# VectorE transposes in place of DRAM bounces, inverses by pairs of blocks, 768-wide weight conversion, and blocks 0 and 1 through the FFN together

## The chip, the cores and the metric

The kernel runs on one core of a Trainium2 chip. The metric is the device time of one execution in microseconds (us); lower is better. TensorE appears in the profile as PE (matmuls) and PEld (loads of the stationary operand), VectorE as DVE, ScalarE as ACT, GpSimd as POOL. SP issues most of the DMAs and ACT issues some; all of them go out through queues to the same 16 DMA engines.

## The reference

Four sequences of 768 tokens with 8 heads of dimension 48 go through a delta rule. For each head, from state 0 (48 x 48) and token by token:

```python
k_n = k / (np.linalg.norm(k, axis=-1, keepdims=True) + 1e-06)
for t in range(S):
    y[:, :, t] = np.einsum('bhd,bhde->bhe', q[:, :, t], state)
    v_old = np.einsum('bhde,bhd->bhe', state, kt)
    state = state + bt[:, :, :, None] * np.einsum('bhd,bhe->bhde', kt, vt - v_old)
```

Then the 3072 outputs of width 384 go through an FFN: `h = x @ w_in` (384 x 2048), a leaky ReLU with slope 0.01, and `@ w_out` (2048 x 384). The weights come as float64, all else as float32.

## The kernel before

**Blocks.** Time is cut into 12 blocks of 64 tokens; a block holds all 32 (sequence, head) pairs, in two groups g of 16. Within a block the recurrence is solved in closed form. `gram(n)` multiplies keys by keys and by queries (tile pg). The key products make, for each of the 32 heads and each half of 32 tokens, a triangular 32 x 32 system L. `norms` and `inv` scale and invert it: `eliminate` takes one of 31 columns per step, with a product into tmp (L263) and a subtraction from T (L268) on VectorE, all 128 partitions at once. `merge` puts the inverses T into the tile rt and builds the coupling of the two halves (matmuls pz and pu). `solve(n)` then runs pk, pw, py (the block's outputs) and pc (the new state). `columns(n)` transposes the outputs into xh and xl, a high and a low part.

**The bounces.** The Gram matrix lies with tokens on partitions, and the inverse needs heads on partitions. So `gram` writes 32 x 32 pieces to DRAM (gd, L209) and reads them back (L, L224). The inverse goes back the same way: td and tt are written (L307, L308) after an ACT copy Tt (L299), and rt and gm are read (L318, L320). For blocks 0 and 1 these DMAs go out on ACT's queue, later on SP's.

**Inverses.** Blocks 0 and 1 are inverted together: two halves times 32 heads times two blocks fill the 128 partitions. Every later block is inverted alone, with the columns of T split over the two halves of the partitions (16 instead of 32 columns, 31 steps).

**FFN.** `ffn(n)` takes the 256 tokens of a block in 16 units f. A unit is nine matmuls ph (w_in chunk f, three splits times three column chunks), an activation gh and ph on ACT (L472, L473), the low part gl on DVE (L475), and six matmuls po with the w_out chunk, two units later.

**Weights.** Each of the 32 half chunks of 384 columns arrives as raw 64-bit words (wr) and is taken apart into a high and a low float by seven DVE operations (L148 to L161) and two ACT ones. Six half chunks are converted ahead of everything else, the other 26 within the FFN of block 0.

**Order.** All of this is Python generators; `weave` says how many steps of solve, inverse, Gram and weights belong to each unit of the FFN, and a scheduler then fixes one order of instructions per engine. Every engine works in that order. Ahead of block n's FFN, its solve must be done; within it run solve(n+1), the inverse of n+2 and the Gram matrix of n+3.

Of the kernel before, what the change touches and what calls it, by code (L numbers as in the profile page):

```python
# [19 lines left out]
D = 48  # L20
C = 64
# [26 lines left out]
def delta_moe_kernel(ctx: ExitStack, tc, kqT, kv, qT, beta, cst, w_all, out, nblk):  # L48
# [33 lines left out]
    NR = dict(k=KT_BUFS, q=Q_BUFS, t=KT_BUFS, v=2 * NGR)  # L82
    ring = {x: [st.tile([P, 2, GU, C if x in "qt" else D], F32, name=f"r{x}{i}") for i in range(NR[x])] for x in NR}
    UP, DN = slice(0, D), slice(R0, P)

    NB = [[0, 1]] + [[n] for n in range(2, nblk)]
    where = {n: (b, i) for b, ns in enumerate(NB) for i, n in enumerate(ns)}

    def of(x, n, g):
        return ring[x][(n * NGR + g) % NR[x]]  # L90

    def statics():
        nc.scalar.dma_start(csb, cst)
        for t in ring["t"]:
            nc.vector.memset(t, 0.0)
        for x in "vq":
            for t in ring[x]:
                nc.gpsimd.memset(t[0:R0], 0.0)
# [27 lines left out]

    def weights():
# [3 lines left out]
        for k in range(2 * NFC):  # L131
            f, x = k // 2, k % 2
            words = raws.pop(k).bitcast(F32).rearrange("p (n two) -> p two n", two=2)
            lo, hi = words[:, 0], words[:, 1]
            loi, hii = lo.bitcast(U32), hi.bitcast(U32)
            g = sb.tile([P, DO], F32, tag="cg", name=f"cg{k}", bufs=CB)
            r = sb.tile([P, DO], F32, tag="cr", name=f"cr{k}", bufs=1)
            gi, ri = g.bitcast(U32), r.bitcast(U32)

            def final():  # L140
                t = sb.tile([P, 2 * DO], F32R, tag=f"w{k}", name=f"w{k}", bufs=1)
                for e in range(2):
# [12 lines left out]
            nc.vector.scalar_tensor_tensor(gi, hii, 0xC0000000, gi, ALU.bitwise_and, ALU.bitwise_or)
            nc.vector.tensor_scalar(ri, hii, 0x1FF, 14, ALU.bitwise_and, ALU.logical_shift_left)
            nc.vector.scalar_tensor_tensor(ri, loi, 18, ri, ALU.logical_shift_right, ALU.bitwise_or)  # L157
            nc.vector.tensor_scalar(e.bitcast(U32), gi, 0xFF800000, None, ALU.bitwise_and)
            d0, d1 = final()
            nc.scalar.copy(d0, g)  # L160
            nc.vector.scalar_tensor_tensor(d1, ri, 2.0 ** -34, e, ALU.mult, ALU.mult)  # L161
# [8 lines left out]
    def dq(n):  # L170

        return nc.scalar if n < 2 else nc.sync


    def gram(n):
        if n * NGR >= Q_BUFS:
            need(sv, solve, n - Q_BUFS // NGR)
        kqs = []
        for g in range(NGR):
            t = sb.tile([P, GS, NPAIR, 2, C], F32, tag="kq", name=f"kq{n}_{g}", bufs=KQ_BUFS)  # L180
            kqs.append(t)
            with behind("L"):
                for b in range(2):
                    (nc.sync, nc.scalar)[b if n < 2 else 0].dma_start(
                        t[b * R0:b * R0 + D].rearrange("p s u x t -> p (s u x t)"), kqT[n, g, b])
        b0, i = where[n]
        if i == 0:
            Lh[b0] = sb.tile([P, HC, HC], F32, tag="L", name=f"L{b0}", bufs=2)
        gd = dr.tile([64, HC, HC], F32, tag="gd", name=f"gd{n}")
# [408 lines left out]
```

## Time and profile before

| quantity | value |
|---|---|
| median of three runs | 725.47 us (725.08 to 725.88) |
| profiled execution: its own span | 722.7 us |
| busy: PE / DVE / ACT / POOL | 625.2 / 499.3 / 323.5 / 7.3 us |
| start to end of the first inverse (blocks 0 and 1) | 43.4 to 64.6 us |
| first matmul ph of the FFN | 95.8 us |
| FFN of block 2 under way | from 230.5 us |
| blocks 3 to 8, one period | 51.3 us |

The profile gives the profiled execution's own time only as its span, from the first to the last instruction; the times of the three runs are measured from outside. The prediction quotes the rows. A row of the groups by line reads: line, engine, operation, out<-in and shape, count, then busy us and mean ns of one, then idle time of the engine just before them and what ended it. A row of the chain of waits reads: start, length, what. A row of the timeline adds engine and line, and in brackets the idle time before. A row of the table by stage reads: stretch, its length, and the busy us of PE, PEld, DVE, ACT, POOL with counts, the granted TensorE clock, the DMA share and GB/s.

### The profile page before, as it was taken

The page shows a single profiled execution, that of the slowest core. Times are in us where ns is not written, and L with a number is a line of the kernel's source. Part 1 is how long each engine was busy: PE and PEld are TensorE (multiplying, and loading weights), DVE is VectorE, ACT ScalarE, POOL GpSimd, SP SyncE. Part 2 cuts the span into 40 slices and gives each one's busy share as a digit, 9 for nine tenths or more (in the row PEclk, how much of TensorE's full clock was granted, in tenths as well). Part 3 has the DMA queues.
Part 4 walks back from the last instruction along what each step waited for, and adds up shares of the span by engine and source line. Part 5 has one row for each costly group of instructions (what it writes and reads, how often), then busy time and mean ns, then how long its engine had stood idle before and what let it go on. Part 6 is the DMA issues. An engine that isn't in the chain of part 4 may idle for free.

```text
span 722.7 us, 20972 instructions
## 1 busy us (share of the span) xinstructions
PE 625.2 (87%) x8296; PEld 580.9 (80%) x8296; DVE 499.3 (69%) x2222; ACT 323.5 (45%) x830; POOL 7.3 (1%) x12
## 2 busy tenths in 40 slices
PE   4200689978996999999999999999999999999996
PEld 4200569967995998988989999989989989999996
DVE  7988998999594856956955947847758559531211
ACT  3211554733453453554454544534634635544332
POOL 4000000000000000000000000000000000000000
PEclk9999978988997999999999999999999999999999
DMA  9594785250306437036055063072171260410000
GB/s 239 102 271 107 177 206 131 59 115 23 46 14 128 85 57 164 4 68 154 3 98 124 3 128 95 15 136 73 32 142 49 50 129 2 68 24 2 3 20 23
DMA packets 130786, 60.91 MB, mean 84 GB/s; under 512 B 115392, under 2 KB 118592, under 8 KB 130688
## 3 DMA queue, kind: packets, MB, share of 16 engines
q1 hardware_dynamic: 117376, 56.81, 35.4%
q10 hardware_dynamic: 13312, 2.76, 2.3%
q8 instruction: 65, 1.06, 0.6%
q14 instruction: 33, 0.27, 0.1%
HBM read 46.96 MB, written 12.58 MB: 82 GB/s over the span
## 4 chain that ended last, share of the span: by engine, by line
PE 65%; DVE 18%; DMA 7%; ACT 4%; SPq 3%; issue 3%; ACTq 0%; DVEq 0%
PE ph L468 26%; PE po L458 23%; PE pw L396 3%; PE pk L383 3%; DVE rq L216 3%; DMA tt<-T 3%; DVE rv L388 2%; DVE T L268 2%; PE pu L342 2%; DVE tmp L263 2%; DMA wr<-in_w_all 2%; PE py L414 2%; PE pz L334 2%; PE px L443 1%; SPq L307 1%
## 5 line engine op out<-in xcount | busy, mean ns | idle before, releaser
L468 PE MATMUL ph<-xh,w 128*128 128x256 f32 x1152 | 255.6, 295 | 11.4 <-DVE gl L475 8.2
L468 PEld LDWEIGHTS ph<-xh,w 128*128 128x128 f32 x1152 | 195.1, 192 | 22.5 <-DVE gl L475 11.4
L458 PE MATMUL po<-w,gh 128*128 128x384 f32 x768 | 188.0, 342 | 2.4 <-ACT gh L472 2.4
L475 DVE TENSOR_TENSOR gl<-ph,gh 128x256 fp32r<-128x256 f32 x192 | 80.4, 422 | 132.4 <-ACT ph L473 123.4
L468 PE MATMUL ph<-xl,w 128*128 128x256 f32 x576 | 165.9, 289 | 1.6 <-DVE xl L116 0.9
L472 ACT ACTIVATE gh<-ph 128x256 fp32r<-128x256 f32 x192 | 73.5, 383 | 171.2 <-PE ph L468 170.1
L458 PEld LDWEIGHTS po<-w,gh 128*128 128x128 f32 x768 | 132.3, 190 | 4.3 <-ACT gh L472 4.0
L458 PE MATMUL po<-w,gl 128*128 128x384 f32 x384 | 118.8, 343 | 1.5 <-DVE gl L475 1.4
L468 PEld LDWEIGHTS ph<-xl,w 128*128 128x128 f32 x576 | 110.7, 192 | 4.4 <-DVE xl L116 3.5
L268 DVE TENSOR_TENSOR T<-T,tmp 128x60 f32<-128x60 f32 (+35 forms) x661 | 112.0, 206 | 1.3
L263 DVE TENSOR_TENSOR tmp<-T,L 128x60 f32<-128x60 f32 (+35 forms) x661 | 111.9, 206 | 0.7
L473 ACT ACTIVATE ph<-ph 128x256 f32<-128x256 f32 x192 | 73.1, 380 | 0.0
L458 PEld LDWEIGHTS po<-w,gl 128*128 128x128 f32 x384 | 68.0, 191 | 2.4 <-DVE gl L475 1.9
L334 PE MATMUL pz<-rt,gm 32*32 32x32 f32 x768 | 19.7, 196 | 39.8 <-DMA rt<-td 39.7
L201 PE MATMUL pg<-kq 48*64 48x128 f32 x768 | 39.8, 313 | 13.2 <-DMA kq<-in_kqT 10.0
L334 PEld LDWEIGHTS pz<-rt,gm 32*32 32x32 f32 x768 | 15.9, 111 | 42.7 <-DMA rt<-td 39.9
L201 PEld LDWEIGHTS pg<-kq 48*64 48x64 f32 x768 | 32.0, 154 | 19.8 <-DMA kq<-in_kqT 10.8
L216 DVE TENSOR_TENSOR rq<-pg,csb 64x256 f32<-64x256 f32 x96 | 40.6, 423 | 2.2 <-ACT gs L205 0.5
L443 PE MATMUL px<-csb,ys 128*128 128x128 f32 x144 | 25.9, 299 | 8.1 <-DVE rq L216 5.1
L160 ACT CAST w<-cg 128x384 fp32r<-128x384 f32 x32 | 16.3, 511 | 36.8 <-DVE cr L157 26.5
L385 ACT ACTIVATE rt<-pk 48x512 f32<-48x512 f32 x44 | 26.1, 593 | 14.2 <-PE pk L383 13.4
L280 DVE MEMSET T<- 128x512 f32 (+1 forms) x11 | 5.8, 524 | 38.1 <-DMA tt<-T 37.9
(61 smaller groups left out, 650.3 us busy)
## 6 DMA issues: line engine op xcount, KB each, us to landing
wr<-in_w_all SPq DMA_DIRECT2D x32, 384.0 KB, 4.9
kq<-in_kqT SPq DMA_DIRECT2D x44, 192.0 KB, 3.6
L<-gd SPq DMA_DIRECT2D x22, 256.0 KB, 3.9
rk<-in_kv SPq DMA_DIRECT2D x24, 192.0 KB, 3.3
rv<-in_kv SPq DMA_DIRECT2D x24, 192.0 KB, 4.2
rq<-in_qT SPq DMA_DIRECT2D x24, 192.0 KB, 3.8
out<-ob SPq DMA_DIRECT2D x48, 96.0 KB, 2.6
gd<-gs SPq DMA_DIRECT2D x88, 32.0 KB, 2.7
```

The costliest lines, as they stand in the source:

```text
L201: nc.tensor.matmul(ps[b][c * 64:(c + 1) * 64, p * 128:(p + 1) * 128], kq[r, c ^ b, p, 0], kq[r, c ^ b, p].rearrange("p x t -> p (x t)"), s ...
L216: nc.vector.tensor_tensor(qa[DN, c, b * NPAIR:(b + 1) * NPAIR], pv[b][r, 1], tri[r].rearrange("p (o t) -> p o t", o=1).broadcast_to([C, NP ...
L263: nc.vector.tensor_tensor(tv, t[:, :, j:j + 1].broadcast_to([P, k, w]), L[:, j, j + 1:].rearrange("p (o w) -> p o w", o=1).broadcast_to([P ...
L268: i = nc.vector.tensor_tensor(t, t, tv, ALU.subtract)
L334: nc.tensor.matmul(zv[h * 64:h * 64 + HC, u], gt[lo, l], t[lo, h, u, HC:], start=True, stop=True)
L385: nc.scalar.mul(t[UP, c], pv[c * 64:c * 64 + D], -1.0)
L443: nc.tensor.matmul(x[:, g * P:(g + 1) * P], ys[n, g][:, cc * P:(cc + 1) * P], eye, start=True, stop=True)
L458: i = nc.tensor.matmul(po[t][:, :DO], a[:, ts_], w[f], start=(f == 0 and k == 0), stop=(f == NFC - 1 and k == 2))
L468: nc.tensor.matmul(ph, a[f][:, cc * P:(cc + 1) * P], x[cc][e], start=(k == 0), stop=(k == 3 * NCC - 1))
L472: nc.scalar.activation(gh, ph, AF.Prelu, alpha=0.01)
L473: i = nc.scalar.activation(ph, ph, AF.Prelu, alpha=0.01)
L475: i = nc.vector.tensor_tensor(gl, ph, gh.bitcast(F32), ALU.subtract)
```

## The change

**Transposes.** The DRAM tiles gd, td and tt and their DMAs are gone. `gram` copies the key products into one SBUF tile S, and `turn` transposes it by 32 x 32 blocks on VectorE into L (four instructions of 32 x 1024 for two blocks). `merge(n)` does the same with T: two such instructions into rt, one into gm. All heads of rt are one tile now. `merge` is one step ahead of the two `join`s, which hold what was left of the old merge.

**Pairs.** Grams and inverses go by pairs of blocks (0,1), (2,3) and so on, six inverses in all, each as wide as the first one was before. The inverse of a pair is laid into the FFN of the even block before it (31 of 33 steps at units 5 to 17), its Gram matrix into units 0 to 4. For the first two pairs the key products come first and the query products (pq) in a second pass, with tiles that lie in weight slots not yet filled.

**Weights.** A chunk f is one load of 768 KB and one conversion 768 wide: seven DVE operations instead of fourteen, two of which work on 16-bit parts of the words. The gates say which conversions may go ahead: behind the first merge for f up to 2, behind block 0's columns for the others. No weight is converted before the first inverse.

**FFN.** Blocks 0 and 1 run together, unit by unit, block 1 four units behind block 0, so that a chunk serves both; the FFN therefore begins with both solves due first, in the order that `weave` gives. Set-up fills and the identity copies move from VectorE to GpSimd.

```diff
-    NR = dict(k=KT_BUFS, q=Q_BUFS, t=KT_BUFS, v=2 * NGR)
+    NR = dict(k=K_BUFS, q=Q_BUFS, v=2 * NGR)
+    rt = st.tile([P, HS, C], F32, name="rt")
...
     def weights():
-        for k in range(2 * NFC):
+        for f in range(NFC):
+            with behind("S0"):
+                nc.scalar.activation(g, hi.bitcast(F32), AF.Abs)
+            with behind(gate):
+                if f >= WU:
+                    nc.vector.tensor_copy(r16[:, 0], part[:, 1])
+                nc.vector.tensor_scalar(r16[:, 1], part[:, 2], 0x1FF, None, ALU.bitwise_and)
+                nc.vector.tensor_scalar(g, g, HI_MIN, HI_MAX, ALU.max, ALU.min)
             nc.vector.tensor_scalar(gi, gi, 3, 0x3FFFF000, ALU.logical_shift_left, ALU.bitwise_and)
+            nc.vector.scalar_tensor_tensor(gi, hi, 0xC0000000, gi, ALU.bitwise_and, ALU.bitwise_or)
+            nc.scalar.copy(t[:, 0:2 * DO], g)
+            nc.vector.tensor_scalar(gi, gi, 0xFF800000, None, ALU.bitwise_and)
+            nc.vector.scalar_tensor_tensor(t[:, 2 * DO:], r, 2.0 ** -36, g, ALU.mult, ALU.mult)
...
+        def turn(parts):
+            for i, n in enumerate(ns):
+                for e in range(2):
+                    r, (S, a) = slice(i * 64 + e * HC, i * 64 + (e + 1) * HC), parts[e]
+                    nc.vector.transpose(L[r], S[r, :, a:a + HC].rearrange("p l t -> p t l"))
...
-                    (nc.sync, nc.scalar)[e if n < 2 else 0].dma_start(
-                        gd[a:a + GU].rearrange("l j i -> j l i"),
...
+    def merge(n):
+        T, gt, a = Ts[n // 2], gm[n], n % 2 * 64
+        for e in (1, 0):
+            nc.vector.transpose(rt[R0 + e * HC:R0 + (e + 1) * HC, :, e * HC:(e + 1) * HC].rearrange("p l i -> p i l"),
+                                T[a + e * HC:a + (e + 1) * HC].rearrange("p m i -> p i m"))
+        d = nc.vector.transpose(gt[0:HC].rearrange("p l m -> p m l"), T[a:a + HC])
...
+    weave(1, (iv, NI, 0, 1))
+    merge(0)
+    weave(NS, (sv, NS, 0, NS), (wg, WF[0], 0, NS))
+    weave(NS, (sv, NS, 0, NS), (gg, 2, 1, NS), (wg, WF[1], 0, NS))
+    columns(1)
...
+    weave(2 * NFC + 1, (wg, NW, 0, W0[0]), (ff, 2 * NFC + 1, 0, 2 * NFC + 1), (iv, NI, *W0[1]), (sv, NS, *W0[2]))
+    for n in range(2, nblk):
+        a, z = n % 2 == 0 and n + 2 < nblk, n % 2 == 1 and n + 1 < nblk
+        weave(NF, (ff, NF, 0, NF), (sv, NS * (n + 1 < nblk), *SV[n % 2]),
+              (gg, NG * a, *GG), (iv, NA * a or (NI - NA) * z, *IV[n % 2]))
+WF = 3, 2
+LAG = 4
+W0 = 26, (0, 18), (20, 30)
```

Three places show how instructions stand now. First, the order on ACT before, behind the end of the first inverse: the copy Tt, the writes td and tt of both blocks, and the reads into rt and gm.

```order
L299 COPY Tt_542<-T_335 128x32x32
L307 DMA td_544<-T_335 32x32x32 x2
L308 DMA tt_545<-Tt_542 32x1024
L307 DMA td_549<-T_335 32x32x32 x2
L308 DMA tt_550<-Tt_542 32x1024
L160 CAST w_831<-cg_818 128x384
L146 ACTIVATE cg_880<-wr_792 128x384
L160 CAST w_847<-cg_834 128x384
L318 DMA rt_81<-td_544 32x16x32
```

The same place on DVE now: the last step of the inverse, three transposes, the start of chunk 0's conversion (cr is the low part, cg the high part, wr the raw words), and the scaling of the values rv.

```order
L331 TENSOR_TENSOR T_381<-T_381,tmp_30_0_580 128x16
L363 STREAM_TRANSPOSE rt<-T_381 32x32x32 x2
L365 STREAM_TRANSPOSE gm_181<-T_381 32x32x32
L139 COPY cr_672<-wr_363 128x768
L140 TENSOR_SCALAR cr_672<-wr_363 128x768
L141 TENSOR_SCALAR cg_671<-cg_671 128x768
L441 TENSOR_TENSOR rv_83<-rv_83,nt_591 64x2x192 x2
```

The ten DMA issues and the copy Tt have no counterpart; three instructions on DVE stand between the inverse and what needs it.

Second, DVE within the joint FFN now: gl_3 with ph_73 is unit 3 of block 1, gl_8 unit 8 of block 0; between them stand parts of the conversions of two chunks and of two elimination steps of blocks 2 and 3.

```order
L547 TENSOR_TENSOR gl_3_1646<-ph_73,gh_3_1645 128x256
L143 SCALAR_TENSOR_TENSOR cg_1726<-wr_1223,cg_1726 128x768
L147 SCALAR_TENSOR_TENSOR w_1632<-cr_1625,cg_1624 128x768
L331 TENSOR_TENSOR T_1251<-T_1251,tmp_8_0_1440 128x5x23
L331 TENSOR_TENSOR T_1251<-T_1251,tmp_9_1_1468 128x5x22
L547 TENSOR_TENSOR gl_8_1678<-ph_72,gh_8_1677 128x256
L139 COPY cr_1727<-wr_1223 128x768
L140 TENSOR_SCALAR cr_1727<-wr_1223 128x768
```

One chunk is converted for two units here, where before two half chunks were converted for one unit.

Third, DVE in the FFN of block 2 now, between the gl of units 5 and 6: the last query products rq of the pair's Gram matrix, the four transposes into L, the corner copies gm.

```order
L547 TENSOR_TENSOR gl_5_2804<-ph_73,gh_5_2803 128x256
L382 COPY zs_1_2701<-pz_1_2700 32x256
L392 TENSOR_SCALAR rt<-pu_0_2678 32x8x32
L392 TENSOR_SCALAR rt<-pu_1_2720 32x8x32
L280 TENSOR_TENSOR rq_80<-pg_1_1_0_2742,csb 64x256
L280 TENSOR_TENSOR rq_82<-pg_1_1_0_2742,csb 64x256
L280 TENSOR_TENSOR rq_80<-pg_1_1_1_2743,csb 64x256
L280 TENSOR_TENSOR rq_82<-pg_1_1_1_2743,csb 64x256
L197 STREAM_TRANSPOSE L_2518<-S_2517 32x1024 x4
L202 COPY gm_2770<-S_2517 32x1024
L202 COPY gm_2772<-S_2517 32x1024
L547 TENSOR_TENSOR gl_6_2848<-ph_72,gh_6_2847 128x256
```

Before, no transposes stood there; the Gram matrix of one block was spread over each block, and DMAs carried it.

More of the change, by code (lines that the diff above doesn't have):

```diff
@@ L268, in eliminate @@
             i = nc.vector.tensor_tensor(t, t, tv, ALU.subtract)
-        if b == 0:
-            mark["inverse"] = i.ins
     def inv(b):
-        for n in NB[b]:
-            need(gg, gram, n)
-        two = len(NB[b]) > 1
-        M = HC if two else HC // 2
-        X = sb.tile([P, HC * HC], F32, tag="T", name=f"T{b}", bufs=1)
-        T = X[:, 0:M * HC].rearrange("p (m i) -> p m i", m=M)
-        nc.vector.memset(T, 0.0)
+        if b > 1:
+            need(gg, gram, b)
+        X = sb.tile([P, HC * HC], F32, tag="S", name=f"T{b}", bufs=1)
+        T = X.rearrange("p (m i) -> p m i", m=HC)
+        if b:
+            with behind("gl"):
+                nc.vector.memset(T, 0.0)
+        else:
+            nc.gpsimd.memset(T, 0.0)
         yield
@@ L324, in merge @@
         lo, r1 = slice(R0 + HC, P), slice(0, HC)
-        if len(NB[where[n][0]]) == 1:
-            r1 = slice(HC, 2 * HC)
-            with behind("h"):
-                nc.scalar.copy(gt[r1].rearrange("p l (m e) -> p l e m", e=2),
-                               gt[0:HC].rearrange("p l (e m) -> p l e m", e=2))
         with behind("po"):
@@ L352, in delta_moe_kernel, with fetch @@
     NSLOT = LD + 3
+    def fetch(n, g):
+        with behind("kq"):
+            for i, x in enumerate("kv"):
+                nc.sync.dma_start(of(x, n, g)[DN].rearrange("p h u t -> p (h u t)"), kv[n, g, i])
+            nc.sync.dma_start(of("q", n, g)[UP].rearrange("p h u t -> p (h u t)"), qT[n, g])
     def solve(n):
-        b, i = where[n]
+        b, i = n // 2, n % 2
         need(iv, inv, b)
@@ L362, in load @@
         def load(g):
-            merge(n, g, of("t", n, g))
-            with behind("L"):
-                for i, x in enumerate("kv"):
-                    nc.sync.dma_start(of(x, n, g)[DN].rearrange("p h u t -> p (h u t)"), kv[n, g, i])
-                nc.sync.dma_start(of("q", n, g)[UP].rearrange("p h u t -> p (h u t)"), qT[n, g])
+            if n and not g:
+                merge(n)
+            join(n, g, of("t", n, g))
+            if n:
+                fetch(n, g)
         def heads(rows):
@@ L387, in kt @@
                 us = slice(s * NPAIR, (s + 1) * NPAIR)
-                nc.vector.tensor_tensor(
+                with behind("inverse" if not n else None):
+                  nc.vector.tensor_tensor(
                     v[DN, :, us], v[DN, :, us],
@@ L484, in ffn @@
             second(*a)
-        for t in range(NTB):
-            ob = sb.tile([P, DO], F32, tag="cg", name=f"ob{n}_{t}", bufs=CB)
-            nc.scalar.copy(ob, po[t][:, :DO])
-            for a in range(0, P, C):
-                r0 = (t * P + a) // C * nblk * C + n * C
-                nc.sync.dma_start(out[r0:r0 + C], ob[a:a + C])
+            if a[1] == NFC - 1:
+                results(a[0])
         yield
```

370 lines of the change are left out of this document (211 added, 159 removed).

## The prediction

> **What bounds the kernel now.** I read the busy lines of the page first: 40 slices of 18 us.
>
> ```profile
> PE   4200689978996999999999999999999999999996
> DVE  7988998999594856956955947847758559531211
> PEclk9999978988997999999999999999999999999999
> ```
>
> From slice 13 on PE is full. Before it DVE is the full one, for ten slices, and PE has holes. A table by stage, cut where the chain of waits changes its owner, says how long each takes:
>
> ```profile
> 0.00:33.50 33.50, 12.82 (x128) 11.04 (x128) 29.19 (x69) 9.51 (x20) 7.35 (x12) 1.00 0.70 167
> 33.50:43.40 9.90, 0.42 (x2) 0.28 (x2) 7.67 (x24) 2.87 (x7) 0.00 (x0) 1.00 1.03 312
> 43.40:64.60 21.20, 0.00 (x0) 0.00 (x0) 21.20 (x131) 0.00 (x0) 0.00 (x0) 1.00 0.49 112
> 64.60:77.40 12.80, 0.03 (x2) 0.03 (x3) 9.71 (x30) 5.53 (x9) 0.00 (x0) 1.00 1.05 220
> 77.40:95.80 18.40, 16.05 (x328) 14.66 (x328) 18.24 (x58) 11.42 (x24) 0.00 (x0) 1.00 0.72 194
> 95.80:182.00 86.20, 75.75 (x850) 68.64 (x851) 80.82 (x304) 43.85 (x114) 0.00 (x0) 0.86 0.40 97
> 182.00:231.50 49.50, 43.15 (x634) 39.65 (x633) 33.44 (x179) 22.08 (x54) 0.00 (x0) 0.91 0.32 53
> 283.70:591.60 307.90, 300.81 (x4212) 278.63 (x4212) 215.21 (x1058) 148.49 (x391) 0.00 (x0) 1.00 0.37 77
> ```
>
> The first inverse is 43.4 to 64.6, DVE alone. From 64.6 to 77.4 PE waits for the bounce (the DMA share is 1.05). Until 182 DVE is 94% busy, with conversions of weights above all. The last row is blocks 3 to 8: 51.3 us each, of which PE idles (307.9 - 300.8) / 6 = 1.2. So the steady part can give at most 1.2 us a block; what there is to win lies ahead of block 2's FFN. The chain of waits names the bounces, there once more at the start of block 2 where PE stood still:
>
> ```profile
> 66.68 4.25 DMA tt<-Tt
> 87.69 2.37 DMA rt<-td
> 220.76 2.50 DMA tt<-T
> ```
>
> In the timeline of that place, DVE idles for the bounce and PE then for DVE; block 2's FFN is under way at 230.5:
>
> ```profile
> 223.57 0.48 DVE L280 MEMSET T<- 128x512 f32 x1 [7.92 <-DMA tt<-T]
> 225.07 2.08 PE L443 MATMUL px<-csb,ys 128*128 128x128 f32 x8 [5.08 <-DVE rq L216]
> 230.55 0.41 PE L468 MATMUL ph<-xh,w 128*128 128x256 f32 x1
> ```
>
> I therefore work out when block 2's FFN starts after the change, and then the steady part.
>
> **Prices.** The groups by line give DVE's operations, and ACT's permuting copy:
>
> ```profile
> L475 DVE TENSOR_TENSOR gl<-ph,gh 128x256 fp32r<-128x256 f32 x192 | 80.4, 422 | 132.4 <-ACT ph L473 123.4 <-PE po L458 6.0
> L388 DVE TENSOR_TENSOR rv<-rv,nt 64x384 f32<-64x384 f32 x48 | 23.8, 555 | 7.9 <-ACT nt L360 7.7
> L292 DVE TENSOR_TENSOR L<-L,cb 128x512 f32<-128x512 f32 x22 | 14.2, 687 | 0.1
> L161 DVE SCALAR_TENSOR_TENSOR w<-cr,ce 128x384 fp32r<-128x384 uint32 x32 | 17.6, 551 | 0.2
> L158 DVE TENSOR_SCALAR ce<-cg 128x384 uint32<-128x384 uint32 x32 | 11.2, 350 | 0.0
> L220 DVE COPY gm<-gs 32x256 f32<-32x256 f32 x48 | 13.8, 288 | 0.7
> L299 ACT COPY Tt<-T 128x1024 f32<-128x1024 f32 x1 | 2.0, 2009 | 22.8 <-DVE T L268 22.8
> 140.00 0.36 DVE L156 TENSOR_SCALAR cr<-wr 128x384 uint32<-128x384 uint32 x1
> 140.27 0.36 DVE L158 TENSOR_SCALAR ce<-cg 128x384 uint32<-128x384 uint32 x1
> ```
>
> With two tensors read, 256 columns take 422 ns and 512 take 687: 1.04 ns a column on a fixed 155. A scalar operation on 384 takes 350, so 0.51 ns a column on the same 155. The last two rows show an instruction starting 0.27 after one of 0.36: independent neighbours overlap by 0.08, so I count each duration less 0.08. A half chunk costs 4 x 0.27 + 3 x 0.47 = 2.49 now, 32 of them 80 us. At 768 columns a scalar operation is 0.155 + 768 x 0.00051 = 0.55, one with a tensor besides 0.95; five and two of them less 7 x 0.08 make 4.1 a chunk, 16 chunks 65 us.
>
> Two prices have no row. **A transpose of 32 x 1024** lies between a plain copy at the rate of L220, 0.155 + 1024 x 0.00052 = 0.69, and ACT's permuting copy of as many columns, 2.01. I take 1.22, one column per 1.04 ns as in DVE's rows with two tensors: the middle of the two ends, and the slower of the two rates that DVE shows. [...] **The two 16-bit operations**, with strides, lie between 0.55 and 0.95; I take 0.55, since L156 and L158, one strided and one not, cost the same. [...]
>
> **The change part by part, up to block 2's FFN.**
>
> *To the first inverse.* The first products now need all key tiles but no weights stand in front of them.
>
> ```profile
> 4.02 1.97 PE L201 MATMUL pg<-kq 48*64 48x128 f32 x16 [4.02 <-DMA kq<-in_kqT]
> 6.91 4.18 PE L201 MATMUL pg<-kq 48*64 48x128 f32 x48 [0.92 <-DMA kq<-in_kqT]
> ```
>
> 128 half-width matmul instructions, at half to all of the second row's 87 ns, from 4.0: done near 10. Then a copy 0.4, four transposes 4.6, eight query products of 512 columns 4.9, the norms, scaling and their dependences 4.6: the inverse starts at 24.8 instead of 43.4. Bounds: 21 to 31. Loads of weights come after the keys, on SP; chunk 0 is not needed before 50. The fills that moved to GpSimd are priced by
>
> ```profile
> L98 POOL MEMSET rq<- 64x1024 f32 x4 | 4.4, 1151 | 0.0
> L98 POOL MEMSET rv<- 64x768 f32 x4 | 2.8, 732 | 0.3 <-POOLq L588 0.3
> ```
>
> 2.3 for rt, four of 0.73, six of 1.15: 12 us from 1 on, then the two identity copies, for which there is no row, and T's fill of 1.15. T is first written by DVE near 23, so the copies have some 4 us each before anything waits; I count nothing.
>
> *The inverse* is what it was: 21.2, to 46.0. *The bounce* of 12.8 becomes three transposes, 3.5: the matmuls pz start at 49.5, not 77.4.
>
> *Solve(0).* On DVE, up to the last xl that the first ph needs, stand 32 instructions: three chunks 12.3, four rv 1.9, three transposes 3.4, a copy 0.6, three xl 1.0, in all 19.2, with 4% for dependences 20. PE and ACT need less, since 18.4 was their time with a DMA wait in it. First ph near 69.5 instead of 95.8: 26 us ahead. The conversions that ran in the first 33 us before are now behind the inverse, which is why it is not 28.
>
> *Solve(1) and the joint FFN.* PE's order sets block 1's px behind the query products pq, and those banks come free when DVE has done 58 more instructions: four transposes 4.6, rv 1.9, 3.4 chunks 14.1, the next norms and scaling 4.3, four products rq 2.4, the rest 1.9, in all 29.2. ACT's cast of chunk 3 stands behind solve(1)'s copies on ACT, and DVE waits for that cast; everything behind it on DVE waits too, I say 4 (0 to 8). With 4% that makes 104. Then up to blocks 2 and 3's merge: 6.6 chunks 27, the inverse 21, 20 gl 6.8, transposes 4.6, products, rv and xl 5.3, in all 64.7, 4% and 3 for waits on gl: 173. PE has only 25 units of work in that stretch (two rows of the timeline where nothing but FFN runs, one unit apart, and one of the chain of waits):
>
> ```profile
> 690.33 0.28 PE L468 MATMUL ph<-xh,w 128*128 128x256 f32 x1
> 692.45 0.28 PE L468 MATMUL ph<-xh,w 128*128 128x256 f32 x1
> 475.25 1.10 PE pg L201 x32
> ```
>
> A unit is 2.12, so 53 us against DVE's 69: DVE sets the end. Behind the merge PE has nine units, 19.1, and solve(2) with px. The steady block gives these: 50.1 busy less 16 x 2.12 less two of the 1.10 for the Gram products, 14. That is 33. PE starts cold: after each hole the granted clock was half for 5 to 11 us, while 120 to 130 has it whole:
>
> ```profile
> 100.00:110.00 10.00, 10.00 (x79) 8.27 (x76) 8.18 (x26) 4.64 (x14) 0.00 (x0) 0.50 0.77 183
> 120.00:130.00 10.00, 10.00 (x169) 9.25 (x168) 9.46 (x33) 5.95 (x15) 0.00 (x0) 1.00 0.28 80
> 225.00:230.00 5.00, 3.88 (x15) 3.28 (x16) 4.78 (x13) 0.55 (x2) 0.00 (x0) 0.50 0.61 94
> ```
>
> I add 3 (0 to 5.5). Block 2's FFN starts at 173 + 33 + 3 = 209, not 230.5: **21.5 us** ahead. So of 28 us won at the first merge 6 are given back, because the joint FFN saves conversion work but hangs on the same DVE.
>
> **The steady part.** PE's instructions per pair are the same, 100.2 us for two blocks without holes. DVE has 61 us of work instead of 72, but it is laid otherwise. Between the gl of unit 5 of the even block and the merge in the odd one it has 45.5 us by the same prices (8.8 with the transposes, 36.7 with norms, inverse, 12 gl and the merge), 47.5 with dependences, while PE has 17 units and solve, 49.5. They are level. I take no gain and no loss. The best case is all 1.2 us of eight blocks, 10; the worst that PE stands at the 8.8 us ahead of unit 6 and at the merge's 4.6, some 4 us for each of four pairs, 16.
>
> **Sum.** 722.7 - 21.5 = 701.2 in the span. The runs' median is 725.47, 2.8 above the span, which I keep: **704**.
>
> **The rivals.** *Transposes dear (slower).* If one costs ACT's 2.01, 0.79 more: 18 of them stand ahead of block 2's FFN, +14; in the steady part eight per pair stand between gl_5 and the merge, 6.3 less the 2 us by which DVE is ahead, 4.3 for four pairs, +17. 704 + 31 = 735. It costs 50 us per us less 8, so the change is even at 0.59 more, 1.8 us a transpose. For it: 4-byte elements and strides on both sides. Against: the fixed rate of all fp32 rows with two tensors. Chance 0.12.
>
> *16-bit operations at one a cycle*: 0.8 for each of the 13 chunks ahead of the merge, 704 + 10 = 714. Chance 0.12.
>
> *The gain does not carry into the steady part*: PE stalls at the bursts, 704 + 16 = 720. For it: gl_6 stands behind 8.8 us, and PE can run two units ahead. Against: query products and solve stand there on PE too. Chance 0.11.
>
> *Better than level*: no waits on ACT and gl (7) and the holes of the block turns filled (7 of 10): 690. For it: DVE has 11 us less per pair. Chance 0.12.
>
> **How the numbers follow.** Forecast 704 with 0.53, its own terms giving 696 to 712. 690, 714 and 720 belong in the range; the dear transposes at 735 lie outside: 686 to 726. A change below about 0.2% (1.5 us) can't be told from none. Faster: 0.53 + 0.12 + 0.12 and most of the 0.11, with something off for sums of mishaps, 0.85; same 0.02; slower 0.13.
>
> **What would show it.** In the changed profile: the inverse starting at 21 to 31 and pz within 5 us of its end; a STREAM_TRANSPOSE row near 1.2 us (above 1.8 the sign turns); L139 and L140 near 0.55; the first ph near 70; DVE full from 50 to 173 with PE holes near 100 and before 173; block 2's FFN near 209; pairs of blocks near 102.6. I am wrong if DVE is not what ends the joint FFN, or if pairs take over 106 or below 100.

## The result: 779.0 us, slower by 7.4%

The changed kernel takes 779.04 us (median of four runs, 776.24 to 782.32), the one before 725.67. The ratio is 1.074, with a 95% interval from 1.071 to 1.077. The forecast was 704, in a range of 686 to 726; the time lies outside, on the other side of the old one. Of all runs below one, of e5_contig (742.1 us), was in the slow state and is left out of its median. The profiled execution has a span of 777.0, 54.3 more than the 722.7 before.

The busy lines of the changed kernel's page, 40 slices of 19.4 us:

```profile
PE   4226958964999898999798999898999798999997
DVE  5999899999434899335998325898325897332121
PEclk9999568995798899899999999999999898999999
```

PE is no longer full behind the front: every second to fourth slice shows an 8 or a 7. The clock row stays at 9 in most of these, because a slice of 19.4 us is long against a fall of the clock to half (in the pair read below 0.50 from 265 to 271 and from 310 to 315); the table by stage, which follows, has its mean. DVE is full only up to slice 9.

```profile
120.00:175.00 55.00, 45.78 (x300) 43.66 (x298) 54.41 (x181) 21.10 (x50) 0.00 (x0) 0.95 0.00 1
182.70:226.70 44.00, 40.66 (x499) 36.86 (x500) 23.91 (x39) 19.30 (x44) 0.00 (x0) 0.77 0.20 47
235.76:581.36 345.60, 321.12 (x4216) 298.52 (x4219) 226.00 (x659) 136.25 (x366) 0.00 (x0) 0.95 0.19 43
```

The last row holds three pairs of blocks: 115.2 us each, against 102.6 before. PE idles (345.6 - 321.1) / 3 = 8.2 in a pair, before 2.4, and it is busy for 107.0 us with as many matmuls as took 100.3 (4216 and 4212 in three pairs). The granted clock is 0.95 instead of 1.00; 100.3 / 0.95 = 105.6, an estimate that lets the busy time go with the clock, and by it the clock is most of the difference.

A mark that every kernel has divides the 54.3: the first xl of block 2, which releases its FFN. It comes at 228.8 before and at 225.8 after. So the front gained 3.0 where 21.5 were forecast, and what follows lost 57.3 (551.2 instead of 493.9) where nothing was forecast. The prices on DVE, from the groups by line:

```profile
L363 DVE STREAM_TRANSPOSE rt<-T 32x1024 f32<-32x1024 f32 x24 | 51.3, 2138 | 10.7 <-PE pw L449 10.2
L197 DVE STREAM_TRANSPOSE L<-S 32x1024 f32<-32x1024 f32 x24 | 46.5, 1939 | 0.5
L365 DVE STREAM_TRANSPOSE gm<-T 32x1024 f32<-32x1024 f32 x12 | 22.7, 1896 | 0.3
L139 DVE COPY cr<-wr 128x768 uint16<-128x768 uint16 x16 | 9.7, 603 | 0.2
```

The 16-bit operations take 0.60 (L140 0.59), about the forecast 0.55. A transpose takes 1.90 to 2.14 and not 1.22: above the 1.8 at which the forecast turned its sign.

**How a pair loses time.** DVE's timeline in the even block of the pair that begins at 235.8, four Gram transposes, two corner copies, and the two gl behind them:

```profile
256.11 7.87 DVE L197 STREAM_TRANSPOSE L<-S 32x1024 f32<-32x1024 f32 x4
264.01 1.39 DVE L202 COPY gm<-S 32x1024 f32<-32x1024 f32 x2
265.43 0.76 DVE L547 TENSOR_TENSOR gl<-ph,gh 128x256 fp32r<-128x256 f32 x2
```

Four products rq stand ahead of them from 254.3, so DVE works 11.1 us in one piece ahead of the next gl. PE's timeline, the table by 3 us, and what PE waited for in the three pairs together (us, times, longest):

```profile
265.91 0.58 PE L540 MATMUL ph<-xh,w 128*128 128x256 f32 x1 [3.46 <-DVE gl L547]
...
260.00:263.00 3.00, 2.45 (x67) 2.07 (x65) 2.97 (x3) 2.50 (x5) 0.00 (x0) 1.00 0.00 0
263.00:266.00 3.00, 0.09 (x1) 0.09 (x1) 2.92 (x5) 0.50 (x2) 0.00 (x0) 0.79 0.00 0
266.00:269.00 3.00, 3.00 (x13) 3.00 (x14) 2.41 (x9) 0.66 (x2) 0.00 (x0) 0.50 0.03 5
269.00:272.00 3.00, 3.00 (x15) 2.90 (x13) 1.71 (x7) 1.10 (x4) 0.00 (x0) 0.58 0.00 0
272.00:275.00 3.00, 3.00 (x29) 2.45 (x27) 2.36 (x12) 0.00 (x0) 0.00 (x0) 1.00 0.04 5
...
PE ph L540 <- DVE gl L547: 15.7, 6, 4.4
PE pu L388 <- DVE gm L365: 6.3, 3, 2.2
```

PE runs two units and the solve's products ahead, stands still for 3.46 us, and then works at half the clock until about 271 (0.50 and 0.58 in the two rows behind 266), which by an estimate, half of the 5 us, costs some 2.5 more. At the odd block's merge, near 310, PE stops again, for another reason first: the solve's products pu need gm, the last of four transposes in one piece (2.1 us a pair), and then comes a wait for gl (1.2 in this pair). The clock is at half there too, from about 309 to 316 (0.51 in 309 to 312, 0.50 in 312 to 315, 0.85 in 315 to 318). In the three pairs gl and gm make 22.0 of the 24.5 us that PE idles.

**How the front loses time.** The table by 5 us around the merge of blocks 2 and 3:

```profile
170.00:175.00 5.00, 0.00 (x0) 0.00 (x0) 4.93 (x35) 0.00 (x0) 0.00 (x0) 0.76 0.00 0
180.00:185.00 5.00, 0.95 (x30) 0.85 (x31) 4.92 (x7) 0.66 (x1) 0.00 (x0) 0.50 0.01 3
195.00:200.00 5.00, 5.00 (x22) 3.70 (x18) 3.50 (x7) 2.15 (x5) 0.00 (x0) 0.50 0.00 0
```

From 169 to 187 PE does almost nothing (3.4 us busy of 18), and then has half the clock until 203 (0.50 in 187 to 203). Its longest wait there is for the merge, whose products pz come next in its fixed order; the units of the FFN that could stand in front of them lack weight chunk 13. SP's own timeline and waits, PE's longest wait from 165 to 205, and the writes of two successive chunks (w, L147) on DVE:

```profile
90.76 4.78 SPq L119 DMA_DIRECT2D wr<-in_w_all  x2
109.60 65.50 SPq L119 DMA_DIRECT2D wr<-in_w_all  x5
...
SPq L119 <- DVE T L331: 62.6, 1, 62.6
PE pz L380 <- DVE rt L363: 7.7, 1, 7.7
...
163.32 0.94 DVE L147 SCALAR_TENSOR_TENSOR w<-cr,cg 128x768 fp32r<-128x768 uint32 x1
189.28 0.96 DVE L147 SCALAR_TENSOR_TENSOR w<-cr,cg 128x768 fp32r<-128x768 uint32 x1
```

The load of chunk 13 waits 62.6 us on SP for the last step of the inverse of blocks 2 and 3, because `gram(1)` puts its tile L into that chunk's slot (tag w13). It is the last load of a chunk on SP: those of chunks 14 and 15 had gone out at 90.8 and 95.2 (first row), when the Gram matrix in their slots had been read. But the chunks are converted in order, so 14 and 15 stand behind 13 on DVE. (The expectation of e6_own_l puts them behind it on SP, which the trace does not bear out.) No chunk is finished between 163 and 189.

### The profile page after: what moved, and what is told of

Same layout as the page of the kernel before. It is cut to its first block, busy times and chain, and to the rows that moved or that the text cites. A ratio compares the mean times of both kernels' runs of the same rounds, so it can differ in the third digit from the quotient of the medians.

```text
span 777.0 us, 20181 instructions
## 1 busy us (share of the span) xinstructions
PE 660.3 (85%) x8552; PEld 617.0 (79%) x8552; DVE 512.7 (66%) x1407; ACT 298.9 (38%) x761; POOL 12.5 (2%) x18
## 4 chain that ended last, share of the span: by engine, by line
PE 64%; DVE 25%; issue 5%; DMA 5%; ACT 1%; SPq 0%; ACTq 0%; DVEq 0%
PE ph L540 25%; PE po L517 21%; DMA kq<-in_kqT 4%; DVE T L331 3%; DVE gm L365 3%; PE pg L272 3%; DVE tmp L326 3%; DVE L L197 3%; PE pw L449 3%; PE pk L435 2%; PE py L467 2%; DVE rt L363 2%; PE pc L457 2%; PE pu L388 2%; PE px L498 2%
## 5 line engine op out<-in xcount | busy, mean ns | idle before, releaser
L540 PE MATMUL ph<-xh,w 128*128 128x256 f32 x1056 | 244.7, 305 | 26.2 <-DVE gl L547 21.9
L540 PEld LDWEIGHTS ph<-xh,w 128*128 128x128 f32 x1056 | 188.8, 203 | 33.5 <-DVE gl L547 23.1
L331 DVE TENSOR_TENSOR T<-T,tmp 128x110 f32<-128x110 f32 (+35 forms) x366 | 76.5, 244 | 0.3
L326 DVE TENSOR_TENSOR tmp<-T,L 128x110 f32<-128x110 f32 (+35 forms) x366 | 76.1, 244 | 0.2
L363 DVE STREAM_TRANSPOSE rt<-T 32x1024 f32<-32x1024 f32 x24 | 51.3, 2138 | 10.7 <-PE pw L449 10.2
L197 DVE STREAM_TRANSPOSE L<-S 32x1024 f32<-32x1024 f32 x24 | 46.5, 1939 | 0.5
L280 DVE TENSOR_TENSOR rq<-pg,csb 64x256 f32<-64x256 f32 x64 | 27.0, 422 | 24.7 <-ACT S L276 23.3
L388 PE MATMUL pu<-zs,gm 32*32 32x32 f32 x768 | 21.9, 204 | 19.5 <-DVE gm L365 14.2
L388 PEld LDWEIGHTS pu<-zs,gm 32*32 32x32 f32 x768 | 18.1, 118 | 25.6 <-issue 15.6
L449 PEld LDWEIGHTS pw<-rv,rt 128*64 128x64 f32 x768 | 28.4, 152 | 7.6 <-issue 6.2
L449 PE MATMUL pw<-rv,rt 128*64 128x48 f32 x768 | 31.3, 238 | 3.2 <-issue 3.2
## 6 DMA issues: line engine op xcount, KB each, us to landing
wr<-in_w_all SPq DMA_DIRECT2D x16, 768.0 KB, 8.7
```

Source lines behind the costliest of these rows:

```text
L197: nc.vector.transpose(L[r], S[r, :, a:a + HC].rearrange("p l t -> p t l"))
L326: nc.vector.tensor_tensor(tv, t[:, :, j:j + 1].broadcast_to([P, k, w]), L[:, j, j + 1:].rearrange("p (o w) -> p o w", o=1).broadcast_to([P ...
L331: i = nc.vector.tensor_tensor(t, t, tv, ALU.subtract)
L363: nc.vector.transpose(rt[R0 + e * HC:R0 + (e + 1) * HC, :, e * HC:(e + 1) * HC].rearrange("p l i -> p i l"), T[a + e * HC:a + (e + 1) * HC ...
L388: nc.tensor.matmul(uv[h * 64:h * 64 + HC, u], gt[r1, l], zs[r1, h, u], start=True, stop=True)
L449: nc.tensor.matmul(pv[r, u], t[:, c, u], v[:, c, u], start=True, stop=True)
```

## The experiments

The table gives each kernel's median, the span of its profiled execution, the first xl of block 2, the time from there to the end, and two pairs (first xl of block 4 to that of 6, and of 6 to that of 8). Within one kernel the span and the median differ by up to 7 us. e1_forms, which only adds instructions at the end, is not in it (one run, 804.2).

| kernel | median | span | xl of block 2 | to the end | pairs |
|---|---|---|---|---|---|
| before | 725.7 | 722.7 | 228.8 | 493.9 | 102.3, 102.6 |
| changed | 779.0 | 777.0 | 225.8 | 551.2 | 112.2, 116.9 |
| e2_copies | 747.5 | 744.1 | 227.9 | 516.2 | 107.8, 105.4 |
| e3_copies_late | 754.2 | 752.1 | 234.4 | 517.7 | 108.0, 107.2 |
| e4_spread | 741.6 | 740.2 | 223.4 | 516.8 | 105.8, 109.0 |
| e5_contig | 734.6 | 737.8 | 214.7 | 523.1 | 107.8, 109.6 |
| e6_own_l | 768.0 | 767.7 | 215.4 | 552.3 | 112.8, 117.2 |
| e7_spread_own_l | 734.2 | 727.5 | 216.5 | 511.0 | 105.5, 105.7 |
| e8_rows | 725.4 | 725.8 | 216.8 | 509.0 | 105.4, 105.8 |
| e9_wu | 725.8 | 723.1 | 216.4 | 506.7 | 105.3, 105.5 |
| e10_lag2 | 731.8 | 730.2 | 220.1 | 510.1 | 104.8, 105.6 |
| e12_all | 732.0 | 730.6 | 219.4 | 511.2 | 107.6, 104.6 |
| e13_kq | 717.0 | 720.2 | 215.4 | 504.8 | 103.6, 103.5 |

### The price of a transpose

```diff
+    A = sb.tile([P, HS, C], F32, tag="S", name="mA", bufs=1)
+    B = sb.tile([P, HC, HC], F32, tag="w0", name="mB", bufs=1)
...
+        nc.vector.transpose(Bf[q], Af[q, 0:1024])
...
+        nc.vector.transpose(B[q], A[q, :, 0:HC].rearrange("p l t -> p t l"))
...
+        nc.vector.transpose(B[q].rearrange("p a b -> p b a"), A[q, :, 0:HC])
+    for _ in range(4):
+        nc.vector.tensor_copy(B[q], A[q, :, 0:HC].rearrange("p l t -> p t l"))
```

> The changed kernel with 40 more instructions at its end, on scratch tiles, four of each form: transposes of 32x1024 float32 with both sides contiguous, 128x1024 contiguous, 32x512 contiguous, 32x1024 and 128x1024 with the strided reading side of the Gram transposes, 32x1024 with a strided writing side; plain VectorE copies of 32x1024 with that strided reading and of 128x1024 contiguous; a GpSimd and a ScalarE copy of 32x1024. Theory A, the price of 1.9 us belongs to a float32 transpose as such: the contiguous 32x1024 takes 1.9 too, 32x512 1.0, 128x1024 1.9. Rival B, the price comes from the strides: the contiguous one takes 0.7 to 1.25, and the strided plain copy is dear as well (over 1.2, where the contiguous copy takes 0.7).

The groups by line at this kernel's end. L616 and L618 transpose in rows, L622 reads with a stride, L626 writes with one; L628 is the plain copy with a strided reading side, L630 the one in rows:

```profile
L616 DVE STREAM_TRANSPOSE mB<-mA 32x1024 f32<-32x1024 f32 x4 | 4.9, 1220 | 0.0
L618 DVE STREAM_TRANSPOSE mB<-mA 128x1024 f32<-128x1024 f32 x4 | 4.9, 1235 | 0.0
L622 DVE STREAM_TRANSPOSE mB<-mA 32x1024 f32<-32x1024 f32 x4 | 8.1, 2012 | 0.0
L626 DVE STREAM_TRANSPOSE mB<-mA 32x1024 f32<-32x1024 f32 x4 | 7.6, 1892 | 0.1
L628 DVE COPY mB<-mA 32x1024 f32<-32x1024 f32 x4 | 4.0, 1012 | 0.1
L630 DVE COPY mB<-mA 128x1024 f32<-128x1024 f32 x4 | 2.8, 694 | 0.1
```

Theory A falls and B holds in the main: in rows a transpose takes 1.22, the forecast's number, and a stride on either side makes it 2.01 (256 bytes reading) or 1.89 (128 writing). A plain copy goes from 0.69 to 1.01, less than the 1.2 that B expected. In rows 32 partitions take 1.22 and 128 take 1.24. All 60 transposes of the changed kernel have a stride.

### Transposes made into copies

```diff
-                    nc.vector.transpose(L[r], S[r, :, a:a + HC].rearrange("p l t -> p t l"))
+                    nc.vector.tensor_copy(L[r], S[r, :, a:a + HC].rearrange("p l t -> p t l"))
...
```

> All 60 transposes are replaced by plain VectorE copies of the same tiles, 0.69 us each by the copies into gm; so that the numbers stay finite the inverse is fed with zero off-diagonals and constant norms by operations of the same widths (what is left out: the transposition and the true inverse). Theory A, the dear transposes do the harm, by delaying gl and through it PE and its clock: with 18 of them ahead of block 2's FFN at 0.53 less than I had counted, the time is 690 to 705 and pairs of blocks take 102 to 104. Rival B, what holds the pairs of blocks is not the transposes (the key loads into the one kq tile, the joint FFN's order, the GpSimd fills): 740 or more, with pairs of 110 or more.

> The same replacement only for the Gram matrices of blocks 4 to 11 and the merges of blocks 3 to 11; the front of the kernel keeps its 10 transposes for blocks 0 to 2 and the four Gram ones of blocks 2 and 3. Theory A, most of the loss lies in the steady part, at 12 us a pair: 777 less 4 x 12 and some 3 at the last blocks, 722 to 732. Rival C, the loss lies ahead of block 2's FFN (the joint FFN and its cold clock) and the steady part only passes it on: above 755.

The edit does the same at the merges and makes the norms constant. 747.5 and 754.2: both above what theory A gave, and the pairs below what B gave. Two things were wrong in the expectations. The copies keep the strides and so cost 1.05 to 1.16 (groups by line of e2_copies), not 0.69:

```profile
L363 DVE COPY rt<-T 32x1024 f32<-32x1024 f32 x24 | 27.7, 1155 | 8.2 <-PE pw L449 7.7
L197 DVE COPY L<-S 32x1024 f32<-32x1024 f32 x24 | 25.2, 1052 | 0.7 <-ACT S L229 0.4
```

And with constant norms the scaling of beta (cb) for the next pair no longer depends on its Gram matrix, so it was put among the steps of the first inverse, where DVE stands and waits for the load of beta (e2_copies; in e3_copies_late 9.5 us):

```profile
47.67 0.18 DVE L310 TENSOR_SCALAR cb<-cb 128x32 f32<-128x32 f32 x1 [9.96 <-DMA cb<-in_beta]
```

The first merge came at 57.8 and 60.2, 9 to 11 us later than in the changed kernel, and the fronts of these two prove nothing. Behind the front both are 33.5 to 35 us faster than the changed kernel, with the late transposes alone replaced too. That points at the transposes, though the order of other work moved as well; a piece of 4.2 + 1.4 + 1.75 us ahead of a gl still leaves some of the loss.

### The same transposes at other places

```diff
-            if (g, c) == steps[-1]:
-                turn([(S, 0), (S, HC)])
-                corners(S)
...
+        pieces = turn([(S, 0), (S, HC)])
+        for x in ((), (0, 1), (), (2, 3)):
+            for i in x:
+                with behind("gl"):
+                    pieces[i]()
+            yield
...
-SV, GG, IV = ((2, 11), (2, 11)), (0, 4), ((5, 17), (0, 1))
-NA = 31
+SV, GG, IV = ((2, 11), (4, 14)), (0, 9), ((9, 17), (0, 4))
+NA = 21
```

> The same instructions and prices as the changed kernel; from block 2's FFN on the transposes stand apart: the four of a Gram matrix in two pairs two units later, the three of an even block's merge one per unit, the gm one of the odd block at the end of the even block's solve; the inverse starts three units later. Theory P, the place: what costs is that more than about 4.2 us of VectorE work stands between two gl in one piece, so PE stops and its clock falls; VectorE has enough idle time for the price itself. Then pairs take 103 to 107 and the time is 732 to 748. Rival A', the price as such: VectorE's 75 us of work per pair set the pace through the chain from Gram to inverse to solve, and the time stays at 770 or more.

741.6, with the same instructions at the same price: 34.4 of the 57.3 lost behind the front come back by the places alone (those of the transposes, and with them those of the Gram products, the solve and the inverse). Theory P holds and rival A' falls: the price as such does not keep a pair at its pace. One of the two pairs, 109.0, is above the expected 107.

### The price at the same places

```diff
-                nc.scalar.copy(S[:, l:l + NPAIR], view[y][:, 0])
+                nc.scalar.copy(S[:, :, l:l + NPAIR].rearrange("p t u -> p u t"), view[y][:, 0])
...
-                    nc.vector.transpose(L[r], S[r, :, a:a + HC].rearrange("p l t -> p t l"))
+                    nc.vector.transpose(L[r], S[r, a:a + HC])
...
-            nc.vector.transpose(rt[R0 + e * HC:R0 + (e + 1) * HC, :, e * HC:(e + 1) * HC].rearrange("p l i -> p i l"),
-                                T[a + e * HC:a + (e + 1) * HC].rearrange("p m i -> p i m"))
+            nc.vector.transpose(rt[R0 + e * HC:R0 + (e + 1) * HC, :, e * HC:(e + 1) * HC],
+                                T[a + e * HC:a + (e + 1) * HC])
...
```

> All transposes of the changed kernel at their places, but with rows of 32 on both sides. For the Gram ones the tile S is kept token by token (ScalarE writes it with a stride, the two corner copies read it with one), which changes no value; the merge ones read and write T, rt and gm as they lie, so the heads and columns of the inverse come to the wrong places (left out: the right placing). The nearest measured row is 1.22 us for a contiguous 32x1024 against 1.9 to 2.1. Theory A, the price: 14 transposes ahead of the merge of blocks 2 and 3 at 0.72 less and four behind it bring block 2's xl from 228 to about 216, and a pair from 115 to 107 to 109, since the piece between two gl shrinks from 11 to about 8.5 us; together 777 - 12 - 4 x 7 - 3 = 734, 725 to 745. Theory P, the place alone: any piece over 4.2 us costs a hole and a cold clock, pairs stay at 112 or more, and the time above 755.

734.6 (730.8 to 739.6), the expected 734: in the profiled run the front gains 11.1, the rest 28.1. The groups by line show the price gone, and where a part of it went (ScalarE's strided writing takes 0.65, in the changed kernel's form 0.38; a corner copy 1.03 instead of 0.69):

```profile
L363 DVE STREAM_TRANSPOSE rt<-T 32x1024 f32<-32x1024 f32 x24 | 29.7, 1238 | 10.6 <-PE pw L449 10.1
L202 DVE COPY gm<-S 32x1024 f32<-32x1024 f32 x10 | 10.3, 1030 | 0.2
L276 ACT COPY S<-pg 128x256 f32<-128x256 f32 x32 | 17.5, 646 | 25.6 <-PE pg L272 23.0 <-PE pn L410 2.6
```

So even at the forecast's own price the kernel is some 10 us slower than the one before (ratio 1.015, with an interval from 1.009 to 1.021): the price is not the only step that failed.

### The load behind the inverse

```diff
-                Lh[b] = L = sb.tile([P, HC, HC], F32, tag="w13", name=f"L{b}", bufs=1)
+                Lh[b] = L = sb.tile([P, HC, HC], F32, tag="L", name=f"L{b}", bufs=1)
```

> One word: the tile L of blocks 2 and 3 lies in L's own slot, which is free by then, and no longer in the slot of weight chunk 13. In the changed kernel the load of chunk 13 waited 62.6 us on SP for the last step of that inverse, and chunks 14 and 15 behind it; PE stood from 169 to 187 and had half the clock until 203. Theory W: that wait is what made the end of the joint FFN 17 us later than I forecast; without it the hole is a third, and block 2's xl comes at 213 to 220 instead of 228: 762 to 770. Rival D: VectorE's work sets the end there anyway (the last conversion is done at 199, after it six units, the solve and the columns): the hole only moves to another place, and the time is 773 or more.

768.0: theory W. Block 2's xl comes 10.4 sooner, and what follows takes as long as before (552.3, 551.2). The conversions of the last three chunks now stand ahead of the merge, which begins at 188.7 instead of 175.0. In this kernel's table by 5 us PE works in the stretch where it had stood still:

```profile
170.00:175.00 5.00, 4.47 (x31) 4.27 (x30) 5.00 (x16) 2.90 (x6) 0.00 (x0) 0.99 0.01 2
185.00:190.00 5.00, 5.00 (x37) 5.00 (x36) 4.57 (x22) 2.51 (x8) 0.00 (x0) 1.00 0.06 14
```

### Both, and the Gram transposes in rows

The next kernel joins the two edits, and the one after it adds the first two diff lines of the price experiment (S token by token; the merges keep their strides).

> The two edits together, transposes spread from block 2's FFN on and L in its own slot, all else as in the changed kernel. They act at different places, so by theory W the gains add: 741.6 less 8 to 15, 726 to 734; by rival D 738 or more.

> The last kernel with the Gram transposes reading rows: S kept token by token, which changes no value (the merges stay strided). 24 of 60 transposes at 1.22 instead of 1.93. Theory A: 8 of them ahead of block 2's FFN give 5.7, and in each of four pairs the four Gram ones 2.8 less in a piece that still costs a small hole, 1 to 2 a pair: 10 us under the last kernel. Rival: ScalarE's writing with a stride and the corner copies (1.0 instead of 0.7) take it back: within 3 us of the last kernel.

734.2 and 725.4. The gains add, and the second kernel is level with the one before the change (ratio 1.001, 0.9995 to 1.003). The 9 us between the two are less sure than they look: of the timed runs of e7_spread_own_l two are at 729 and two at 739 to 740, and the two profiled spans differ by 1.7. What is sure is that the front did not move (216.5, 216.8), though by the expectation it had 5.7 to gain. DVE's timeline in e8_rows shows where that went:

```profile
98.21 0.56 DVE L146 TENSOR_SCALAR cg<-cg 128x768 uint32<-128x768 uint32 x1 [3.19 <-ACT w L145]
```

By 95 DVE is 3.7 us ahead of e7_spread_own_l, and then it waits for ScalarE's cast of a chunk (w, L145); chunk 3 is written at 98.8 instead of 99.2, and the merge begins at 189.2 instead of 189.5.

### Less work on VectorE in the front

```diff
-WA, WU = 3, 0
+WA, WU = 3, 16
...
-LAG = 4
+LAG = 2
...
-                (nc.vector.tensor_copy if b else nc.scalar.copy)(gm[n][R0 + HC:P], S[i * 64 + HC:(i + 1) * 64, 0:HC].rearrange("p t l -> p l t"))
+                nc.scalar.copy(gm[n][R0 + HC:P], S[i * 64 + HC:(i + 1) * 64, 0:HC].rearrange("p t l -> p l t"))
```

> The last kernel (transposes spread, Gram ones by rows, L in its own slot) with the 16-bit copy L139 of every chunk on ScalarE instead of VectorE: 16 x 0.60 = 9.6 us less on VectorE, of which some 8 lie between the first merge and the last conversion. Theory D, VectorE's sum of work sets the end of the joint FFN: block 2's xl comes 6 to 9 us sooner than 217, and the time is 715 to 720. Rival: ScalarE, with about 0.9 a copy more in front of gh and of the cast, or the solve of block 2 on PE, sets that end: 723 or more.

> The same with block 1 two units behind block 0 instead of four. Behind the last conversion two units fewer are left, 4.2 us by 2.12 each, while PE waits for block 1's columns two units earlier in a stretch where VectorE is full. By theory D only what stands behind VectorE's last work counts: 2 to 4 us under the kernel with the 16-bit copies on ScalarE. Rival: the earlier wait delays block 0's units and their gl, 0 to 4 us slower.

> Both, and the corner copies (L202, 1.07 us each with the strided reading, two behind each Gram transposition) on ScalarE. From the pieces between two gl 2.1 us go, once a pair, where a hole of 1 to 2 us is left: 0 to 8 us under the kernel with two units of lag, 706 to 716; rival: ScalarE's gh, which then stands behind two copies of about 1.0, stops PE as well: no gain.

The first line alone gives 725.8, no change, as theory D's rival had it. The merge of block 2 does come 5.8 us sooner (183.4 instead of 189.2), but block 2's xl does not (216.4). Theory D itself was put to half a test only: the last conversion ended at 182.1 instead of 183.6, 1.5 sooner and not 8. DVE's waits from 180 to 225, and PE in that stretch, of e9_wu:

```profile
DVE rt L375 <- PE pw L466: 6.7, 1, 6.7
...
195.00:200.00 5.00, 5.00 (x90) 4.71 (x90) 1.93 (x5) 2.62 (x8) 0.00 (x0) 0.96 0.36 82
200.00:205.00 5.00, 5.00 (x84) 4.45 (x84) 0.85 (x2) 2.22 (x5) 0.00 (x0) 1.00 0.59 118
```

With L in its own slot PE is the one that ends last there: it is full from 195, DVE is not. PE in turn is held before that by the merge's four transposes, which still stand in one piece (4.0 us of waiting for gl). Two units of lag make it 6 us slower, more than the 4 that its rival allowed, from a cause that was not followed; the corner copies on ScalarE change nothing in the sum (731.8, 732.0).

### The last wait in a pair

In e8_rows a pair has one hole of more than 0.5 us left, at the first group's second step. PE's timeline and the table by 3 us:

```profile
337.82 1.09 PE L273 MATMUL pg<-kq 48*64 48x128 f32 x18 [1.04 <-DMA kq<-in_kqT]
...
335.00:338.00 3.00, 1.96 (x23) 1.49 (x23) 0.17 (x1) 0.00 (x0) 0.00 (x0) 1.00 0.25 38
338.00:341.00 3.00, 3.00 (x57) 2.89 (x55) 1.39 (x4) 1.56 (x4) 0.00 (x0) 0.70 0.00 0
341.00:344.00 3.00, 3.00 (x19) 3.00 (x18) 2.94 (x7) 0.83 (x3) 0.00 (x0) 0.73 0.01 3
```

```diff
-            t = sb.tile([P, 2, 2, GS, NPAIR, C], F32, tag="kq", name=f"kq{b}_{g}", bufs=1)
+            for c in range(2):
+                t = sb.tile([P, 2, 2, NPAIR, C], F32, tag=f"kq{c}", name=f"kq{b}_{g}_{c}", bufs=1)
...
```

> The kernel with spread transposes, Gram ones by rows and L in its own slot, and one edit more: the kq tile is two tiles of half the size, one for each of the two steps of a group, so the next group's load starts after the first step's products and not after both. In that kernel a pair takes 105.4 against 102.6 before; in the pair PE waits 1.2 us for the kq load, and the clock is low for some 5 us behind it, about 3 us a pair in all. Theory K: this wait is what is left of the loss per pair; without it pairs take 102.6 to 103.5 and the time is 713 to 719, less than both kernels. Rival: twice as many DMAs of half the size on SP, with runs of 1 KB, come no sooner, or the hole comes back at the next gl: 722 or more.

717.0 (712.4 to 722.0), the fastest of all: ratio to the kernel before 0.988, with an interval from 0.985 to 0.991, a gain of 1.2%. The profiled run is the slowest of the six. PE's waits from 330 to 640 and its table row for the pair from 330:

```profile
PE ph L563 <- DVE gl L570: 1.8, 3, 1.4
...
330.00:433.00 103.00, 102.67 (x1402) 94.72 (x1402) 73.30 (x219) 46.42 (x122) 0.00 (x0) 1.00 0.20 48
```

The wait for kq is gone, and the clock is whole.

## Why the prediction was wrong

Between the forecast span, 701.2, and the measured 777.0 lie 75.8 us: 18.5 in the front and 57.3 behind it.

**To the first inverse, right in kind.** It ends at 48.8 and not 46.0: four transposes at 1.93 are 2.8 more, which is the whole difference. The inverse itself takes its 21 us, and pz starts 2.0 behind its end. Chunk conversions and 16-bit operations were priced right: seven operations of 0.55 to 0.95, less their overlaps, are 4.2 us. (No run shows a rate by the cycle: the rival's "at one a cycle" comes to 0.95 instead of 0.55 for each of two operations, the author's estimate, and 0.60 and 0.59 were measured.)

**"I take 1.22 ... the middle of the two ends, and the slower of the two rates that DVE shows": wrong.** 1.9 to 2.1. The rows that set the price had no stride; the instruction has strides on one side or both, and the row that had them, ACT's permuting copy at 2.01, was the nearest. (Nor is 1.22 the middle of 0.69 and 2.01; that is 1.35.) By e5_contig the price costs 11.1 us in the front and 28.1 behind it, net of the dearer copies around it; the 28.1 and the 34.4 of the places overlap, since together they are more than the 57.3 lost. (By e1_forms a stride adds 0.7 to 0.8 us to a transpose of 1024 elements, which then lie 128 or 256 bytes apart, and 0.3 to a plain copy. Why it does is not shown.)

**"They are level. I take no gain and no loss": wrong, and the larger error.** I compared sums over half a pair, 47.5 us of DVE against 49.5 of PE. But PE can run only two units and what the solve puts between them ahead of a gl; work that DVE could do elsewhere in the half pair does not help when 11.1 us stand in one piece. The sum itself was sized about right: DVE is busy 53.8 us in the changed kernel from 251.0 to 311.4, of which the dearer price of eight transposes is some 6 to 7, and 45.5 were forecast. Here it was not the sum that set the pace but the longest piece ahead of a result that PE waits for (gl, and gm at the merge). The kernel with the transposes spread shows it with equal sums. At the forecast's price a pair still takes 5 to 7 us more than before (e5_contig), more than the 4 that the rival of the steady bursts took as its worst; some 2 of that are the wait for kq, by e8_rows and e13_kq.

**The clock was counted once, it falls in every pair.** I added 3 us at the first merge, on the ground that after each hole the clock was half. The trace of before does not show that of each hole: behind PE's longest wait, 39.7 us up to 77.4, the clock is 1.00 from 77.4 to 95.8, by the forecast's own table. In the pairs 5.8 of the 12.6 lost are idle time and 6.8 are longer busy time, most of it by the clock (0.95, the estimate above). (Not all: e13_kq is busy 102.7 us in a pair at a clock of 1.00, the kernel before 100.3.) The rival of the dear transposes names the right price, but gave 735 and not 779: it counted 4.3 a pair, from sums again.

**"PE has nine units, 19.1, and solve(2)" behind the merge: a wait was overlooked.** The merge began at 175.0, the forecast 173. But block 2's FFN followed it at 226, 51 and not 36 later, since chunk 13 was not there. The tile tags in the code show that wait, and the forecast did not follow them: by e6_own_l it is 10.4 of the 15 us; the rest was not divided further. These 10.4 and the 11.1 of the price can't be added: each edit alone brings the xl to about 215 (215.4, 214.7), and with L in its own slot the Gram transposes in rows gave nothing more. (The forecast's own terms give 174, not 173.)

**Right:** DVE nearly full from 49 to 183, and PE holes near 100 and before 173. The first ph came at 76.7 instead of 69.5, with six strided transposes (some 4.5) and the late inverse (2.8) ahead of it. The 4 us for ScalarE's cast were 1.8 here, and 4.1 in e8_rows. That the merge began at 175.0 all the same, near the forecast, is in part luck: 7 us were lost up to the first ph, and 5 came back between it and the merge.

**Open.** Even the fastest kernel needs 504.8 from block 2's xl to the end in its profiled run, 10.9 more than before. By the first xl of each block, 3.9 of it lie between blocks 2 and 4, 2.2 between 4 and 8, and 4.8 between 8 and 11. Between 4 and 8 it is hardly waiting: in the pair from 330 PE is busy 102.67 of 103.00 us. Between 8 and 11 stand 1954 matmuls instead of 1890, as many more as one block's Gram matrix has. Further it was not followed. Whether one transpose over 128 partitions could do the work of four, as the near prices in rows suggest (1.22 and 1.24), was not tried.

## What to carry to other kernels

Before a stall is removed by work on an engine that is not the bound, ask how long that work stands in one piece in front of the next result that the bounding engine waits for, and how far that engine can run ahead; the sum over a stage doesn't answer it. An instruction's price is taken from a row with its own access pattern. And where a tile borrows the slot of a later load, that load waits for the tile's last reader (here 62.6 us), and with it all work that a fixed order puts behind the loaded data.

## What the runs showed of the hardware

A transpose of float32 in rows takes 1.22 us for 32x1024 and 1.24 for 128x1024, and with a stride on one side 1.89 to 2.01 for 32x1024 (e1_forms); the transposes of the changed kernel take 1.90 to 2.14. A hole of 3.46 us in PE was followed by about 5 us at half the clock (changed kernel, 0.50 in 266 to 269, 0.58 in 269 to 272). A hole of only 1.04 us, amid products of 48 rows, was followed by two stretches of 3 us with a mean clock of 0.70 and 0.73 (e8_rows), which by an estimate is (0.30 + 0.27) x 3 / 0.5, some 3.4 us, at half; without the hole, in e13_kq, the clock is 1.00 over the pair from 330. Whether the small products beside the hole have a part in it, no run here tells.
